# RWKV5 attention and a SwiGLU block: k and r without padding, a pair of heads in 96 columns, and zeros from a scale column

## The chip, the cores and the metric

The kernel runs on one core of one Trainium2 chip. The metric is the device time of one execution in microseconds (us), as the median over several executions. The span that a profile shows is about 1.7 us shorter than the time measured for the same execution, because it runs from the first to the last instruction. The granted clock is the share of its full speed at which TensorE was allowed to run, as the profile reports it.

Engines are named as in the profile: PE is TensorE's matmul stream, PEld its weight loads, DVE is VectorE, ACT is ScalarE, POOL is GpSimd and SP issues DMA. "L226" is a line of the kernel's source. Adding lines moves the numbers, so the same statement has other numbers in other kernels: `khat` is L226 before and L225 after.

## The reference

```python
B, H, S, D = 4, 8, 768, 48                    # r, k, v: (B, H, S, D); w, u: (H, D); all float32
for t in range(S):
    kt, vt, rt = k[:, :, t], v[:, :, t], r[:, :, t]
    cur = einsum('bhd,bhe->bhde', u[None] * kt, vt)
    y[:, :, t] = einsum('bhd,bhde->bhe', rt, state + cur)
    state = w[None, :, :, None] * state + einsum('bhd,bhe->bhde', kt, vt)
x = y.transpose(0, 2, 1, 3).reshape(B * S, H * D)              # 3072 x 384
g = x @ w_gate                                                 # 384 x 1536
out = (g * sigmoid(g) * (x @ w_val)) @ w_out                   # 1536 x 384
```

## The kernel before

The kernel cuts the sequence into chunks of 128 tokens. One step handles one chunk of one batch, 24 steps in all. Within a chunk the recurrence becomes matrix products: `khat` is k times a power of the decay, `rhat` is r divided by such a power, the scores are their product under a triangular mask, and the state `Z` is updated once a chunk. The term with `u` touches only the diagonal: `du` is the sum of r·k·u over a head, and `At` starts as the identity times `du`, before the scores are copied into it under the mask. Two heads go through TensorE together. Beside the steps runs the FFN (lines `gv` and `o_ps`), and in the first steps the FFN's weights, which arrive as 64-bit words, are rounded on ScalarE, VectorE and GpSimd.

Each head's 48 columns are padded to 64, so that a pair fills 128 columns, and after the transpose 128 partitions. The transposed k of each head sits in its own half of a tile `kT`, whose other half is zeroed once, at the start.

```python
    DP = 64                                   # D is 48, P is 128, H is 8, HP is 4
    wcol = cst.tile([P, HP], FP32, name="wcol")
    kscale = cst.tile([P, H, DP], FP32, name="kscale")
    r_ld = [cst.tile([P, H, DP], FP32, name=f"r_ld{i}") for i in range(2)]
    khat = [cst.tile([P, H, DP], FP32, name=f"khat{i}") for i in range(4)]
    kT = [cst.tile([P, HP, 2, P], FP32, name=f"kT{i}") for i in range(2)]
    # ... (cut) set-up:
    dve.tensor_scalar(held[:], wcol[:], W_LOW, W_HIGH, ALU.max, ALU.min)
    dve.tensor_copy(sq[:, 0, :], held[:])
    # ... (cut) powers of the decay by squaring, reciprocal, transposes into kscale and rscale
    for t in kT:
        for e in range(2):
            pool.memset(t[64 * e : 64 * e + 64, :, 1 - e, :], 0.0)

    def round_weights(count):                 # (cut) per chunk of weights:
            dve.tensor_scalar(dst, hi, -(1 << 31), None, ALU.bitwise_and)
            dve.scalar_tensor_tensor(dst, mag, 3, dst, ALU.logical_shift_left, ALU.bitwise_or)
            pool.tensor_tensor(dst, dst, low, ALU.add)

    def prepare(i):
        # ... (cut)
        pool.tensor_mul(khat[i % 4][:], kl[:], kscale[:])
        pool.tensor_mul(rhat[i % 2][:], rl[:], rscale[:])
        pool.tensor_mul(rk[:], rl[:, :, 0:D], kl[:, :, 0:D])
        pool.tensor_mul(rk[:], rk[:], ub[:])
        dve.tensor_reduce(du[:], rk[:], axis=AX.X, op=ALU.add)

    def turn(i):
        for nm, t in (("kT", khat[i % 4]), ("rT", rhat[i % 2])):
            tp = ps_a.tile([P, HP, P], FP32, name="tp", tag="a")
            for a in range(HP):
                pe.transpose(tp[:, a, :], t[:, 2 * a : 2 * a + 2, :].rearrange("p e d -> p (e d)"), ident[:])
            if nm == "kT":
                for e in range(2):
                    q = slice(64 * e, 64 * e + 64)
                    act.copy(kT[i % 2][q, :, e, :], tp[q])
            # ... (cut)

    def update(i):
        # ... (cut)
        for a in range(HP):
            pe.matmul(
                ps[:, a, :].rearrange("p (e d) -> p e d", e=2),
                kh[:, 2 * a : 2 * a + 2, :].rearrange("p e d -> p (e d)"),     # the weights
                v_pair(a),                                                     # (shortened) 2 x 48 columns of v
                start=True, stop=True, skip_group_check=True)

    prepare(0)
    for s in range(N + 2):                    # (cut: how many FFN pieces go in between)
        if 1 <= s <= N: diagonal(s - 1)       # At = ident * du, on GpSimd
        if s + 1 < N:   prepare(s + 1)
        if s < N:       turn(s)
        round_weights(1 if s else 0)
        # scores(s - 1), outputs(s - 2), update(s - 2)
        round_weights(1 if s > 1 else 0)
```

The order of instructions on each engine is fixed by this program order.

## Time and profile before

| what | value |
|---|---|
| time, median of 4 executions | 755.26 us (754.04 to 755.65) |
| span of the profiled execution | 752.1 us |
| PE busy | 704.4 us, 94% |
| POOL busy | 203.6 us, 27% |

The prediction below shows the page's shares, the chain and the windows of this kernel. Three more readings are kept here, because they are compared later.

The first is the timeline of the set-up of the kernel before: start us, duration us, engine, line, operation, tiles; in brackets the idle time before it and what ended that.

```profile
2.23 2.19 POOL L210 MEMSET kT<- 64x512 f32 x4
3.39 0.49 DVE L178 TENSOR_SCALAR held<-wcol 128x4 f32<-128x4 f32 x1 [1.60 <-DMA wcol<-in_w_dram]
3.92 0.52 DVE L179 COPY sq<-held 128x4 f32<-128x4 f32 x1
```

The two VectorE instructions touch four columns and last half a microsecond each. While they ran, GpSimd was filling `kT`.

The second is the chain of waits around the first state update after the start-up, and the transposes that follow it (start us, us, what):

```profile
142.73 0.86 PE u_ps L306 x8
...
146.21 0.87 PE tp L248 x8
```

Eight of each cost the same there. The third is the duration (min/median/max ns) of ScalarE's copies into `kT` between 130 and 740 us:

```profile
L254 ACT COPY kT<-tp x30: 579/580/582, 146.7 to 624.8; 64x512 f32<-64x512 f32 x30
```

### The profile page before, as it was taken

How to read it: one execution, taken by the hardware profiler on the slowest of the kernel's cores; microseconds unless marked ns; L12 is line 12 of the kernel's file. 1: busy time of each engine (PE TensorE's matmuls, PEld its weight loads, DVE VectorE, ACT ScalarE, POOL GpSimd, SP SyncE). 2: the span in 40 equal slices, each digit the busy share in tenths (PEclk: the TensorE clock that was granted, in tenths of full speed). 3: DMA queues.
4: the chain of work that ended last, by engine and by line, in shares of the span. 5: the costliest groups of instructions: out<-in, count | busy, mean ns of one | idle time of the engine just before them, and what ended most of it. 6: DMA issues, size and time to landing. Idle time of an engine off the chain costs nothing.

```text
span 752.1 us, 10222 instructions
## 1 busy us (share of the span) xinstructions
PE 704.4 (94%) x4298; PEld 563.0 (75%) x4298; DVE 218.1 (29%) x448; ACT 153.9 (20%) x305; POOL 203.6 (27%) x168
## 2 busy tenths in 40 slices
PE   2775978999999999999999999999999999999997
PEld 1654867878878778778778778778778778777773
DVE  4255654523222222223123213123213212212120
ACT  2541634311112111102111112111112112111110
POOL 5865667650303030303030303030302311000000
PEclk9988989999999999999999999999999999999999
DMA  8565555121102020102020201020100000000000
GB/s 213 112 152 147 165 161 156 32 43 33 32 11 43 1 43 11 31 11 43 1 53 1 44 11 31 12 42 5 38 22 1 23 12 2 12 10 2 10 11 24
DMA packets 85767, 33.98 MB, mean 45 GB/s; under 512 B 76368, under 2 KB 79568, under 8 KB 85712
## 3 DMA queue, kind: packets, MB, share of 16 engines
q1 hardware_dynamic: 82256, 28.52, 16.2%
q10 hardware_dynamic: 3456, 4.72, 1.8%
q8 instruction: 36, 0.59, 0.3%
q14 instruction: 19, 0.16, 0.1%
HBM read 28.51 MB, written 4.72 MB: 44 GB/s over the span
## 4 chain that ended last, share of the span: by engine, by line
PE 85%; POOL 6%; DVE 5%; issue 2%; ACT 1%; DMA 0%; SPq 0%; DVEq 0%; POOLq 0%
PE gv L332 48%; PE o_ps L351 25%; PE y_ps L293 4%; PE s_ps L263 4%; PE tp L248 2%; PE u_ps L306 2%; POOL At L239 2%; POOL rhat L227 1%; POOL khat L226 1%; POOL rk L229 1%; POOL rk L228 1%; DVE wv L156 1%; DVE wg L156 1%; DVE wv L155 1%; DVE wg L155 1%
## 5 line engine op out<-in xcount | busy, mean ns | idle before, releaser
L332 PE MATMUL gv<-xT,wg 128*128 128x256 f32 x864 | 217.5, 389 | 19.1 <-DVE hT L340 16.8
L332 PE MATMUL gv<-xT,wv 128*128 128x256 f32 x864 | 212.7, 383 | 0.0
L332 PEld LDWEIGHTS gv<-xT,wg 128*128 128x128 f32 x864 | 161.5, 193 | 50.4 <-issue 20.0
L351 PE MATMUL o_ps<-wo,hT 128*128 128x384 f32 x576 | 197.4, 487 | 0.6 <-ACT o_sb L357 0.6
L332 PEld LDWEIGHTS gv<-xT,wv 128*128 128x128 f32 x864 | 166.7, 193 | 23.5
L339 DVE TENSOR_TENSOR sg<-sg,gv 128x256 f32<-128x256 f32 x144 | 60.5, 420 | 359.3 <-ACT sg L338 359.3
L351 PEld LDWEIGHTS o_ps<-wo,hT 128*128 128x128 f32 x576 | 107.7, 190 | 62.0 <-ACT o_sb L357 1.2
L338 ACT ACTIVATE sg<-gv 128x256 f32<-128x256 f32 x144 | 55.3, 384 | 427.2 <-PE gv L332 427.2
L319 POOL TENSOR_TENSOR Z<-Z,wL 128x384 f32<-128x384 f32 x16 | 16.5, 1032 | 342.2 <-DVE Z L318 342.2
L340 DVE TENSOR_TENSOR hT<-sg,gv 128x256 f32<-128x256 f32 x144 | 60.5, 420 | 4.9
L239 POOL TENSOR_TENSOR At<-ident,du 128x1024 f32<-128x1024 f32 x24 | 45.5, 1898 | 37.6 <-PE y_ps L293 37.6
L263 PEld LDWEIGHTS s_ps<-rT,kT 128*128 128x128 f32 x384 | 50.4, 197 | 7.0 <-DVE At L267 0.7
L263 PE MATMUL s_ps<-rT,kT 128*128 128x128 f32 x384 | 51.0, 281 | 0.3 <-DVE At L267 0.3
L267 DVE COPY_PREDICATED At<-mask,s_ps 128x512 f32<-128x512 int32 x48 | 34.0, 732 | 41.5 <-PE s_ps L263 41.5
L231 DVE TENSOR_REDUCE du<-rk 128x8 f32<-128x384 f32 x24 | 13.3, 553 | 100.0 <-POOL rk L229 100.0
L293 PE MATMUL y_ps<-At,v_ld 128*32 128x128 f32 x768 | 36.7, 283 | 5.2 <-issue 2.8
L293 PEld LDWEIGHTS y_ps<-At,v_ld 128*32 128x32 f32 x768 | 30.4, 113 | 6.5 <-issue 3.6
L226 POOL TENSOR_TENSOR khat<-k_ld,kscale 128x512 f32<-128x512 f32 x24 | 30.5, 1271 | 5.4 <-ACT kscale L195 5.4
L227 POOL TENSOR_TENSOR rhat<-r_ld,rscale 128x512 f32<-128x512 f32 x24 | 30.6, 1274 | 2.0 <-ACT outside L218 2.0
L254 ACT COPY kT<-tp 64x512 f32<-64x512 f32 x48 | 27.9, 580 | 12.6 <-PE tp L248 11.3
L293 PE MATMUL y_ps<-rT,Z 128*32 128x128 f32 x480 | 30.1, 279 | 0.0
L293 PEld LDWEIGHTS y_ps<-rT,Z 128*32 128x32 f32 x480 | 19.3, 109 | 8.3 <-issue 7.8
(60 smaller groups left out, 318.4 us busy)
## 6 DMA issues: line engine op xcount, KB each, us to landing
k_ld<-in_k_dram SPq DMA_DIRECT2D x24, 192.0 KB, 3.1
r_ld<-in_r_dram SPq DMA_DIRECT2D x24, 192.0 KB, 3.5
w_bits<-in_moe_w_gate_dram SPq DMA_DIRECT2D x6, 768.0 KB, 4.6
w_bits<-in_moe_w_val_dram SPq DMA_DIRECT2D x6, 768.0 KB, 4.6
v_ld<-in_v_dram SPq DMA_DIRECT2D x48, 96.0 KB, 2.7
w_bits<-in_moe_w_out_dram SPq DMA_DIRECT2D x6, 768.0 KB, 4.3
out_dram<-o_sb ACTq DMA_DIRECT2D x24, 192.0 KB, 1.9
ub<-in_u_dram SPq DMA_DIRECT2D x1, 192.0 KB, 4.5
```

Of the source, the lines that this page charges most:

```text
L226: pool.tensor_mul(khat[i % 4][:], kl[:], kscale[:])
L227: pool.tensor_mul(rhat[i % 2][:], rl[:], rscale[:])
L239: pool.tensor_mul(At[i % 2][:], ident[:].unsqueeze(1).to_broadcast([P, H, P]), dus.pop(i)[:].unsqueeze(2).to_broadcast([P, H, P]),)
L254: act.copy(kT[i % 2][q, :, e, :], tp[q])
L263: pe.matmul(ps[:, n, :], kT[i % 2][:, a, e, :], turned[i][:, a, :], start=True, stop=True, skip_group_check=True,)
L267: dve.copy_predicated(At[i % 2][:, 4 * half : 4 * half + 4], mask[:].bitcast(INT32).unsqueeze(1).to_broadcast([P, HP, P]), ps[:],)
L293: pe.matmul(ps[32 * q : 32 * q + 32, cc, :], *rows[q][n], start=(n == 0), stop=(n == len(rows[q]) - 1), skip_group_check=True,)
L332: pe.matmul(gv[:, o, :].rearrange("p (i t) -> p i t", i=2), wt[:, c, P * f : P * (f + 1)], xT[:, 2 * g % NX : 2 * g % NX + 2, c, :], start ...
L338: act.activation(sg[:], gv[:, 0, :], AF.Sigmoid)
L339: dve.tensor_mul(sg[:], sg[:], gv[:, 0, :])
L340: dve.tensor_mul(hT[g][:, f, :], sg[:], gv[:, 1, :])
L351: pe.matmul(ps[:], hT[g][:, f, P * j : P * (j + 1)], wo[:, f, :], start=(f == 0), stop=(f == FC - 1),)
```

## The change

The padding goes: k, r and their scales are 8 x 48 = 384 columns wide, a pair of heads is 96 columns and 96 partitions. Then the two heads of a pair no longer start at partitions 0 and 64 but at 0 and 48. Instead of copying each half into a pre-zeroed tile, ScalarE copies all 96 rows twice, each time scaled by a column that is 1 on the rows of one head and 0 on the others. The memsets of `kT` go with it. The core of the diff:

```diff
-    kscale = cst.tile([P, H, DP], FP32, name="kscale")
+    kscale = cst.tile([P, H, D], FP32, name="kscale")
+    own = cst.tile([D2, 2], FP32, name="own")                 # D2 = 96
-    khat = [cst.tile([P, H, DP], FP32, name=f"khat{i}") for i in range(4)]
+    khat = [cst.tile([P, H, D], FP32, name=f"khat{i}") for i in range(4)]
-    kT = [cst.tile([P, HP, 2, P], FP32, name=f"kT{i}") for i in range(2)]
+    kT = [cst.tile([D2, HP, 2, P], FP32, name=f"kT{i}") for i in range(2)]
 ... (r_ld, k_ld, rhat, wcol, held, sq, Z, wL and the powers likewise; cut)
+    pool.memset(own[:], 1.0)
+    for step, base in ((-D, 0), (D, D - 1)):
+        pool.affine_select(
+            out=own[:], in_=own[:], compare_op=ALU.is_ge, fill=0.0,
+            base=base, pattern=[[step, 2]], channel_multiplier=1 if step < 0 else -1,
+        )
-    for t in kT:
-        for e in range(2):
-            pool.memset(t[64 * e : 64 * e + 64, :, 1 - e, :], 0.0)
 ... (cut)
                 for e in range(2):
-                    q = slice(64 * e, 64 * e + 64)
-                    act.copy(kT[i % 2][q, :, e, :], tp[q])
+                    act.activation(
+                        kT[i % 2][:, :, e, :], tp[0:D2], AF.Identity, scale=own[:, e : e + 1]
+                    )
 ... (cut)
-        ps = ps_a.tile([P, HP, 2 * D], FP32, name="u_ps", tag="a")
+        ps = ps_a.tile([D2, HP, D2], FP32, name="u_ps", tag="a")
         for a in range(HP):
             pe.matmul(
                 ps[:, a, :].rearrange("p (e d) -> p e d", e=2),
-                kh[:, 2 * a : 2 * a + 2, :].rearrange("p e d -> p (e d)"),
+                pair(kh, a),                                   # the same two heads, now 96 columns
```

More of the change, by code (lines that the diff above doesn't have):

```diff
@@ L49, in fast @@
     B, H, S, D = r.shape
-    DP = 64
+    D2 = 2 * D
     VW = 2 * D + 16
@@ L64, in fast @@
     dve, pool, act, pe, sp = nc.vector, nc.gpsimd, nc.scalar, nc.tensor, nc.sync
-    wcol = cst.tile([P, HP], FP32, name="wcol")
+    wcol = cst.tile([D2, HP], FP32, name="wcol")
     ub = cst.tile([P, H, D], FP32, name="ub")
-    kscale = cst.tile([P, H, DP], FP32, name="kscale")
-    rscale = cst.tile([P, H, DP], FP32, name="rscale")
-    wL = cst.tile([P, HP, 2 * D], FP32, name="wL")
-    sq = cst.tile([P, 8, HP], FP32, name="sq")
-    bad = cst.tile([P, HP], FP32, name="bad")
-    held = cst.tile([P, HP], FP32, name="held")
-    badc = cst.tile([P, 1], FP32, name="badc")
-    ones = cst.tile([P, 1], FP32, name="ones")
+    kscale = cst.tile([P, H, D], FP32, name="kscale")
+    rscale = cst.tile([P, H, D], FP32, name="rscale")
+    own = cst.tile([D2, 2], FP32, name="own")
+    wL = cst.tile([D2, HP, 2, D], FP32, name="wL")
+    sq = cst.tile([D2, 8, HP], FP32, name="sq")
+    bad = cst.tile([D2, HP], FP32, name="bad")
+    held = cst.tile([D2, HP], FP32, name="held")
+    badc = cst.tile([D2, 1], FP32, name="badc")
+    ones = cst.tile([D2, 1], FP32, name="ones")
     ident = cst.tile([P, P], FP32, name="ident")
@@ L83, in fast @@
     xT = cst.tile([P, NX, CC, P], FP32, name="xT")
-    Z = [cst.tile([P, HP, 2 * D], FP32, name=f"Z{b}") for b in range(B)]
-    r_ld = [cst.tile([P, H, DP], FP32, name=f"r_ld{i}") for i in range(2)]
-    k_ld = [cst.tile([P, H, DP], FP32, name=f"k_ld{i}") for i in range(2)]
+    Z = [cst.tile([D2, HP, D2], FP32, name=f"Z{b}") for b in range(B)]
+    r_ld = [cst.tile([P, H, D], FP32, name=f"r_ld{i}") for i in range(2)]
+    k_ld = [cst.tile([P, H, D], FP32, name=f"k_ld{i}") for i in range(2)]
     v_ld = [cst.tile([P, HP, VW], FP32, name=f"v_ld{i}") for i in range(4)]
-    khat = [cst.tile([P, H, DP], FP32, name=f"khat{i}") for i in range(4)]
-    rhat = [cst.tile([P, H, DP], FP32, name=f"rhat{i}") for i in range(2)]
+    khat = [cst.tile([P, H, D], FP32, name=f"khat{i}") for i in range(4)]
+    rhat = [cst.tile([P, H, D], FP32, name=f"rhat{i}") for i in range(2)]
     At = [cst.tile([P, H, P], FP32, name=f"At{i}") for i in range(2)]
-    kT = [cst.tile([P, HP, 2, P], FP32, name=f"kT{i}") for i in range(2)]
+    kT = [cst.tile([D2, HP, 2, P], FP32, name=f"kT{i}") for i in range(2)]
     def load(i):
@@ L98, in load @@
         for src, dst in ((k, k_ld[i % 2]), (r, r_ld[i % 2])):
-            sp.dma_start(out=dst[:, :, 0:D], in_=src[b, :, rows, :].rearrange("h t d -> t h d"))
+            sp.dma_start(out=dst[:], in_=src[b, :, rows, :].rearrange("h t d -> t h d"))
     def load_v(i):
@@ L158, in round_weights @@
             load_weights()
-    pool.memset(wcol[:], 1.0)
-    for t in k_ld + r_ld:
-        dve.memset(t[:, :, D:DP], 0.0)
     for t in v_ld:
@@ L166, in fast @@
     for e in range(2):
-        sp.dma_start(out=wcol[64 * e : 64 * e + D, :], in_=w.rearrange("(a e) d -> e d a", e=2)[e])
+        sp.dma_start(out=wcol[D * e : D * e + D, :], in_=w.rearrange("(a e) d -> e d a", e=2)[e])
     load(0)
@@ L181, in fast @@
         dve.tensor_mul(sq[:, l, :], sq[:, l - 1, :], sq[:, l - 1, :])
-    pw = two.tile([P, HP, P + 1], FP32, name="pw", tag="hT")
-    ipw = two.tile([P, HP, P], FP32, name="ipw", tag="hT")
+    pw = two.tile([D2, HP, P + 1], FP32, name="pw", tag="hT")
+    ipw = two.tile([D2, HP, P], FP32, name="ipw", tag="hT")
     dve.memset(pw[:, :, P : P + 1], 1.0)
@@ L187, in fast @@
         n = 1 << l
-        f = sq[:, l, :].unsqueeze(2).to_broadcast([P, HP, n])
+        f = sq[:, l, :].unsqueeze(2).to_broadcast([D2, HP, n])
         dve.tensor_mul(pw[:, :, P - 2 * n : P - n], pw[:, :, P - n : P], f)
@@ L191, in fast @@
     for src, dst in ((pw[:, :, 1 : P + 1], kscale), (ipw[:], rscale)):
-        t_ps = ps_a.tile([P, HP, P], FP32, name="t_ps", tag="a")
+        t_ps = ps_a.tile([P, HP, D2], FP32, name="t_ps", tag="a")
         for a in range(HP):
-            pe.transpose(t_ps[:, a, :], src[:, a, :], ident[:])
+            pe.transpose(t_ps[:, a, :], src[:, a, :], ident[0:D2, 0:D2])
         act.copy(dst[:].rearrange("p h d -> p (h d)"), t_ps[:].rearrange("p a x -> p (a x)"))
-    pool.memset(wL[:], 0.0)
-    for e in range(2):
-        q = slice(64 * e, 64 * e + 64)
-        dve.tensor_copy(
-            wL[q, :, D * e : D * (e + 1)], sq[q, 7, :].unsqueeze(2).to_broadcast([64, HP, D])
-        )
+    dve.tensor_mul(
+        wL[:], sq[:, 7, :].unsqueeze(2).unsqueeze(3).to_broadcast([D2, HP, 2, D]),
+        own[:].unsqueeze(1).unsqueeze(3).to_broadcast([D2, HP, 2, D]),
+    )
     pool.memset(mask[:], 1.0)
@@ L207, in fast @@
     )
-    for t in kT:
-        for e in range(2):
-            pool.memset(t[64 * e : 64 * e + 64, :, 1 - e, :], 0.0)
     dve.tensor_tensor(bad[:], held[:], wcol[:], ALU.not_equal)
@@ L227, in prepare @@
         pool.tensor_mul(rhat[i % 2][:], rl[:], rscale[:])
-        pool.tensor_mul(rk[:], rl[:, :, 0:D], kl[:, :, 0:D])
+        pool.tensor_mul(rk[:], rl[:], kl[:])
         pool.tensor_mul(rk[:], rk[:], ub[:])
@@ L242, in diagonal, with pair @@
         )
+    def pair(t, a):
+        return t[:, 2 * a : 2 * a + 2, :].rearrange("p e d -> p (e d)")
     def turn(i):
@@ L247, in turn @@
             for a in range(HP):
-                pe.transpose(
-                    tp[:, a, :], t[:, 2 * a : 2 * a + 2, :].rearrange("p e d -> p (e d)"), ident[:]
-                )
+                pe.transpose(tp[0:D2, a, :], pair(t, a), ident[:])
             if nm == "kT":
                 for e in range(2):
-                    q = slice(64 * e, 64 * e + 64)
-                    act.copy(kT[i % 2][q, :, e, :], tp[q])
-            else:
-                turned[i] = three.tile([P, HP, P], FP32, name=nm, tag=nm)
-                act.copy(turned[i][:], tp[:])
+                    act.activation(
+                        kT[i % 2][:, :, e, :], tp[0:D2], AF.Identity, scale=own[:, e : e + 1]
+                    )
+            else:
+                turned[i] = three.tile([D2, HP, P], FP32, name=nm, tag=nm)
+                act.copy(turned[i][:], tp[0:D2])
     def scores(i, half):
@@ L315, in update @@
         if c == 0:
-            dve.tensor_mul(z[:], ps[:], wL[:])
+            dve.tensor_mul(z[:], ps[:], wL[:].rearrange("p a e d -> p a (e d)"))
         else:
             dve.tensor_add(z[:], ps[:], z[:])
-            pool.tensor_mul(z[:], z[:], wL[:])
+            pool.tensor_mul(z[:], z[:], wL[:].rearrange("p a e d -> p a (e d)"))
     hT = {}
```

## The prediction

> **What bounds the kernel now.** I read the page first, for the engines' shares and the chain that ended last, then the table of windows, then the chain in order of time for the first 150 us, then the waits, and last the instruction durations of single lines. The page says TensorE is busy nearly all the time, but not where the rest of the chain lies:
>
> ```profile
> PE 704.4 (94%) x4298; PEld 563.0 (75%) x4298; DVE 218.1 (29%) x448; ACT 153.9 (20%) x305; POOL 203.6 (27%) x168
> ...
> PE 85%; POOL 6%; DVE 5%; issue 2%; ACT 1%; DMA 0%; SPq 0%; DVEq 0%; POOLq 0%
> ```
>
> So about 13% of the span, some 100 us, is chain that is not TensorE. The table of windows (width; then busy us of PE, PEld, DVE, ACT and POOL, with counts; granted clock; DMA share; GB/s) says where:
>
> ```profile
> 50.00:60.00 10.00, 7.46 (x34) 6.10 (x35) 6.66 (x10) 3.79 (x6) 5.45 (x5) 0.83 0.59 147
> 60.00:70.00 10.00, 4.46 (x51) 3.53 (x50) 2.91 (x5) 2.45 (x4) 7.27 (x7) 0.92 0.50 117
> ...
> 300.00:400.00 100.00, 100.00 (x559) 79.64 (x558) 25.39 (x56) 16.19 (x36) 21.81 (x18) 1.00 0.12 26
> ```
>
> Before about 105 us TensorE starves; from about 125 us on it never does. The kernel is two stages with different bounds. In the first, the chain in order of time (start us, us, what) repeats this cycle, about 14.4 us long where no TensorE piece joins it:
>
> ```profile
> 46.07 1.90 POOL At L239
> 47.97 1.22 POOL khat L226
> 49.19 1.22 POOL rhat L227
> 50.41 0.97 POOL rk L228
> ...
> 51.45 1.00 POOL rk L229
> 52.48 0.55 DVE du L231
> 53.03 0.87 DVE wv L155
> ```
>
> After it come the rest of the weight rounding on VectorE, one weight add on GpSimd (POOL, L157), and the next `At`. The waits of the same stage (16 to 105 us: total, times, longest) confirm that VectorE waits for POOL in every cycle, so each microsecond of those five POOL products is on the path:
>
> ```profile
> DVE du L231 <- POOL rk L229: 50.7, 8, 8.3
> ```
>
> In the second stage the chain is TensorE back to back, and only TensorE's pitch counts. Durations of two of its lines there (142 to 200 us; min/median/max ns):
>
> ```profile
> L306 PEld LDWEIGHTS u_ps<-v_ld,khat x24: 190/192/192, 142.4 to 195.5; 128*128 128x128 f32 x24
> L306 PE MATMUL u_ps<-v_ld,khat x24: 246/275/275, 142.6 to 195.6; 128*128 128x96 f32 x24
> L248 PEld LDWEIGHTS tp<-ident,khat x8: 140/140/142, 145.7 to 164.6; 128*128 128x128 f32 x8
> ```
>
> **What the Trainium skill says.** "TensorE: Matmul & The Clock Gate", the section on LDWEIGHTS: a weight load's time goes with its columns, P/1.2 ns, and not with the contraction rows. The trace agrees: 128 columns take a median of 192 ns here (u_ps) and the 32-column loads of y_ps 109 to 110, so 82 ns for 96 columns, 0.86 ns each. "GPSIMD Engine Reference", section 3.1: a two-input product is bound by one shared read port at about 2.5 cycles of a 1.2 GHz clock per element. The trace agrees: 512 columns take 1272 ns (khat, rhat), 384 take 1000 (rk), so 2.1 ns a column. "ScalarE: Activation LUTs", "What ACT_TABLE_LOAD costs": an ACTIVATE pays about 93 ns for each per-partition pointer operand; no run so far shows it. The same page, "Table sets", puts identity in every set; the changed program indeed has the same two table loads.
>
> **The change part by part.**
>
> (1) `khat` and `rhat` shrink from 512 to 384 columns. Their step in the chain should fall from 1.23 us to that of `rk`, 0.965: 0.265 us each, 0.53 us a cycle. In the first stage the pairs that start at 16.4, 22.7, 33.5, 48.0, 62.4, 78.4 and 97.3 us are on the chain, and the very first `rhat` too: 7 x 0.53 + 0.27 = **4.0 us** on the path. Later pairs lie beside TensorE: nothing.
>
> (2) The set-up. Four POOL memsets of kT (2.19 us), that of wL (0.42) and VectorE's four of k and r (0.6) go; POOL stood idle 5.38 us before the first `khat`, so that gives nothing. On the chain are: the memset of wcol ahead of its load (about 0.15 us by the start times; the other engines start at 0.8), the four transposes of the second scale, 96 columns moved in place of 128 at the cold pitch of about 0.22 us a transpose (1.09 to about 0.87), and ScalarE's copy (0.587 to the 0.479 of another 384-column copy). Together **0.45 us**. The reciprocal (3.35 us) keeps 512 columns a partition.
>
> (3) The state update (L306) loads 96 columns of weights in place of 128. Eight instructions take 0.86 us on the chain, 108 ns each, although only 96 columns move; the score products with 128 moved columns take 1.78 us for 16, 111 ns. So I take the update to be bound by its weight load (its matmuls show a median of 275 ns against a minimum of 246, which I read as waiting for weights). With 96 columns both sides come to about 80 to 84 ns: 24 to 26 ns an instruction, 0.2 us an update. 20 updates exist, 5 run before 105 us; 15 x 0.2 = **3.0 us** on the path.
>
> (4) The transposes (L248, 8 in 0.87 us, 109 ns each) also load 96 columns, but their load is shorter already, 140 ns against 192, and they still move 128 columns of the identity. I count **0**. Score and output products contract 96 rows in place of 128, at the same columns: **0**. Tile shapes are unchanged in the program (128 by 128 and 128 by 32), so no new switch of mode.
>
> (5) `kT` goes from 48 ScalarE copies of 64x512 (580 ns) to 48 scaled copies of 96x512. Perhaps +93 ns each, 4.5 us of ScalarE work. Its reader is the score product of the *next* step, a cycle of 14 to 18 us later, and ScalarE is 20% busy: **0** on the path.
>
> (6) The loads of k and r carry the same bytes from the same 192-byte rows; DMA lies off the chain (0%).
>
> Sum: 4.0 + 0.45 + 3.0 = 7.5 us; 755.1 - 7.5 = 747.6. I round to **747.8**.
>
> **Rivals.** *A, the POOL saving is not passed on.* If VectorE's fixed order made a score product or a weight load the wait that ends last, `du` would start earlier and the masked copy after it would wait instead. For it: VectorE's order is fixed, and ScalarE's rounding copies also wait on VectorE. Against: the score products are done about 1.7 us before their masked copies (38.8 and 40.5 us), and they move up with `rhat`. Then 751. *B, transposes are bound by their weight load.* If 96 columns help there too, each of some 120 later transposes gains up to 27 ns, 3.2 us more: 744.5. Against: the 140 ns load. *C, the update is bound by something else* (a fixed pitch near 108 ns, say): part 3 is nothing, 750.7. For it: no 96-column load exists in this trace. *D, the clock.* Three TensorE pieces of the first stage ran at a lower granted clock: 12 instructions of gv took 5.23, 4.89 and 4.21 us instead of 2.6 to 2.9. Shifting the idle time moves where such a window falls, some 2 us either way. *E, ScalarE becomes a wait*: it would need to lose a whole cycle of slack; I give it little.
>
> **Range and chances.** The largest doubts are D (2 us), B (-3) and A or C (+3 each). That makes a standard deviation near 3 us: range **744.0 to 752.0**. Faster by over 2% means below 740.0, which needs more than twice the sum; 0.02. Slower by over 2% needs a new stall of 15 us; 0.01. Within 2%: 0.97.
>
> **What would show it.** In the changed profile: khat and rhat near 1.0 us each and a first-stage cycle near 13.9 us in place of 14.4; TensorE back to back from about 100 us on; the update's weight load near 165 ns and eight of its instructions in about 0.66 us; transposes still 0.87 us for eight; kT copies of 0.58 to 0.68 us with nobody waiting for them. The prediction is wrong if the cycle keeps 14.4 us with a new releaser (A), if the update's eight keep 0.86 (C), if the transposes' eight fall to about 0.66 (B), or if the score or output products get slower with 96 rows, which I count as nothing.

## The result, and the profile after

The changed kernel took 746.19 us (median of 4, 746.14 to 746.27) against 755.26 us. The ratio is 0.9883, with a 95% interval of 0.9866 to 0.9900: within 2%, as predicted, and inside the range. A ratio here is the mean time of one kernel's fast runs over that of the other's of the same rounds, so it is not quite the ratio of the medians. The results are correct.

The page of the kernel after, first the engines' busy time, then the shares of the chain that ended last:

```profile
PE 699.4 (94%) x4298; PEld 557.3 (75%) x4298; DVE 216.7 (29%) x443; ACT 152.8 (21%) x305; POOL 188.2 (25%) x165
...
PE 83%; POOL 7%; DVE 6%; issue 3%; ACT 1%; DMA 0%; SPq 0%; DVEq 0%; POOLq 0%
```

POOL lost 15.4 us of work and PE 5.0 us, and the span fell by 7.7 us (752.1 to 744.4): neither engine's busy time gives the answer, since most of POOL's work lay beside TensorE. The shape of the chain has not changed.

The chain of the kernel after in one cycle of the start-up stage:

```profile
42.89 1.89 POOL At L238
44.78 0.95 POOL khat L225
45.73 0.95 POOL rhat L226
46.69 0.97 POOL rk L227
...
47.72 1.01 POOL rk L228
...
48.75 0.55 DVE du L230
```

`khat` and `rhat` now take a step of 0.95 us each instead of 1.22. The next `At` starts at 56.77 us: the cycle is 13.9 us, where it was 14.4. It has the same members in the same order. The waits between 16 and 105 us (total us, times, longest us) name the same releaser:

```profile
DVE du L230 <- POOL rk L228: 42.5, 7, 7.8
```

Before, the same wait was 50.7 us over 8 times. The timeline of the set-up of the kernel after:

```profile
3.23 0.17 DVE L183 TENSOR_SCALAR held<-wcol 96x4 f32<-96x4 f32 x1 [2.01 <-DMA wcol<-in_w_dram]
3.43 0.17 DVE L184 COPY sq<-held 96x4 f32<-96x4 f32 x1
```

The two small VectorE instructions take 0.17 us each in place of 0.49 and 0.52. No GpSimd memset runs beside them any more.

Then the durations between 130 and 740 us (min/median/max ns), of the update's weight loads and products, the transposes' loads and the scaled copies:

```profile
L307 PEld LDWEIGHTS u_ps<-v_ld,khat x112: 163/165/165, 137.1 to 575.0; 128*96 128x96 f32 x112
L307 PE MATMUL u_ps<-v_ld,khat x112: 246/248/248, 137.3 to 575.0; 128*96 128x96 f32 x112
...
L250 PEld LDWEIGHTS tp<-ident,khat x60: 124/126/129, 140.3 to 616.1; 128*96 128x96 f32 x60
...
L253 ACT ACTIVATE kT<-tp,own x30: 671/677/683, 141.3 to 617.2; 96x512 f32<-96x512 f32 x30
```

And the same two pieces of the chain as shown of before:

```profile
137.50 0.68 PE u_ps L307 x8
...
140.78 0.87 PE tp L250 x8
```

The update's eight instructions fell from 0.86 to 0.68 us; the eight transposes still take 0.87 us, although their weight load is shorter too.

Laying the two traces side by side along the chain gives a ledger for the whole 7.7 us of span. The first `rhat` starts at 11.82 us instead of 13.06: 1.24 us from the set-up. The eighth of the start-up's `At` starts at 124.47 instead of 130.01: 5.54 us, so 4.30 came from the eight cycles in between. The next `y_ps` starts at 133.01 instead of 138.25: 5.24 us, so 0.30 was given back there: the twelve `gv` instructions in between took 4.51 us instead of 4.21. From it to the end the gain grows to 7.7 us, so 2.46 came from the stretch where TensorE runs back to back and 14 updates of 0.18 us less (2.52 us) lie.

### The profile page after: what moved, and what is told of

Its sections match the earlier page's. It is cut to its first block, busy times and chain, and to the rows that moved or that the text cites. A ratio compares the mean times of both kernels' runs of the same rounds, so it can differ in the third digit from the quotient of the medians.

```text
span 744.4 us, 10214 instructions
## 1 busy us (share of the span) xinstructions
PE 699.4 (94%) x4298; PEld 557.3 (75%) x4298; DVE 216.7 (29%) x443; ACT 152.8 (21%) x305; POOL 188.2 (25%) x165
## 4 chain that ended last, share of the span: by engine, by line
PE 83%; POOL 7%; DVE 6%; issue 3%; ACT 1%; DMA 0%; SPq 0%; DVEq 0%; POOLq 0%
PE gv L333 47%; PE o_ps L352 25%; PE y_ps L294 4%; PE s_ps L264 4%; PE tp L250 2%; POOL At L238 2%; PE u_ps L307 1%; POOL rk L228 1%; POOL rk L227 1%; POOL khat L225 1%; POOL rhat L226 1%; DVE At L268 1%; DVE wg L157 1%; DVE wg L156 1%; DVE wv L157 1%
## 5 line engine op out<-in xcount | busy, mean ns | idle before, releaser
L320 POOL TENSOR_TENSOR Z<-Z,wL 96x384 f32<-96x384 f32 x16 | 16.4, 1028 | 348.0 <-DVE Z L319 348.0
L264 PEld LDWEIGHTS s_ps<-rT,kT 96*128 96x128 f32 x384 | 49.9, 196 | 7.6 <-ACT kT L253 0.8
L264 PE MATMUL s_ps<-rT,kT 96*128 96x128 f32 x384 | 50.5, 279 | 0.8 <-ACT kT L253 0.5
L253 ACT ACTIVATE kT<-tp,own 96x512 f32<-96x512 f32 x48 | 30.2, 677 | 11.4 <-PE tp L250 10.4
L294 PE MATMUL y_ps<-rT,Z 96*32 96x128 f32 x480 | 30.2, 278 | 0.0
L294 PEld LDWEIGHTS y_ps<-rT,Z 96*32 96x32 f32 x480 | 19.3, 109 | 8.3 <-issue 7.8
L225 POOL TENSOR_TENSOR khat<-k_ld,kscale 128x384 f32<-128x384 f32 x24 | 23.8, 993 | 6.1 <-ACT kscale L200 6.1
L358 ACT COPY o_sb<-o_ps 128x384 f32<-128x384 f32 x24 | 11.5, 478 | 64.7 <-PE o_ps L352 64.7
```

What stands on the lines that cost most here:

```text
L253: act.activation(kT[i % 2][:, :, e, :], tp[0:D2], AF.Identity, scale=own[:, e : e + 1])
L264: pe.matmul(ps[:, n, :], kT[i % 2][:, a, e, :], turned[i][:, a, :], start=True, stop=True, skip_group_check=True,)
L294: pe.matmul(ps[32 * q : 32 * q + 32, cc, :], *rows[q][n], start=(n == 0), stop=(n == len(rows[q]) - 1), skip_group_check=True,)
L320: pool.tensor_mul(z[:], z[:], wL[:].rearrange("p a e d -> p a (e d)"))
```

## The experiments

Twelve runs were made, in three groups that each shared executions of the kernel before on the same chip (medians of it 755.19, 754.94 and 754.05 us). Unless it says otherwise, the ratio is against the kernel before. Theory: the gain is the sum of the update's narrower loads, the narrower GpSimd products, and the set-up. The rivals are those of the prediction: a part of the sum is worth nothing, or the gain is the clock.

### The changed kernel once more

No edit; it is the control for the runs on the same chip.

> The changed kernel once more, as the control of this set. First measured ratio 0.988 (746.2 us). Both theories (the gain is the shorter GpSimd products plus a shorter set-up plus the narrower weight load of the update; or mostly a luckier fall of the granted clock) expect 0.986 to 0.991 here; the second also allows another value on another chip.

Measured: 745.55 us (744.90 to 746.21), ratio 0.9880 [0.9865, 0.9895]. The executions fall into two groups, at 744.9 and 746.2 us; so do those of the kernel before, at 754.1 and 755.3. The profiled execution was of the lower group, the one of the result above was not, and they can be compared. Their chains agree up to 118.1 us. The next twelve FFN instructions, first of the kernel after in the upper group, then of this run in the lower one:

```profile
118.07 4.51 PE gv L333 x12
```

```profile
118.11 2.83 PE gv L333 x12
```

The update that follows starts at 137.50 us in the one and at 136.27 in the other, 1.23 us apart. The granted clock from 118 to 123 us is 0.66 in the one and 1.00 in the other. So between these two executions the spacing of the groups is whether TensorE's lower granted clock falls on these instructions. A difference of about one microsecond between two medians can be no more than which group the executions fell into; for such a size the trace is read instead.

### GpSimd products over 512 columns again

The products `khat` and `rhat` run over 512 contiguous columns (128 of them padding, zeroed once by VectorE in the set-up), everything else stays as in the kernel after.

```diff
-        pool.tensor_mul(khat[i % 4][:], kl[:], kscale[:])
-        pool.tensor_mul(rhat[i % 2][:], rl[:], rscale[:])
+        pool.tensor_mul(khat_w[i % 4][:], k_w[i % 2][:], kscale_w[:])      # tiles of 512 columns,
+        pool.tensor_mul(rhat_w[i % 2][:], r_w[i % 2][:], rscale_w[:])      # used through views of 384
```

> The changed kernel with the two GpSimd products khat and rhat made over 512 columns a partition again (128 columns of zeros behind the 384), all else as changed. Theory: eight pairs and the first rhat lie on the chain of the first stage, 0.27 us a product, so 4.2 to 4.8 us come back: about 750.6 us, ratio to the kernel before 0.994; the cycle goes from 13.9 to 14.4 us. Rival (the products are hidden and the gain is elsewhere): 746 us.

Measured: 750.94 us (750.87 to 751.98), ratio 0.9954 [0.9940, 0.9967]; 5.6 us more than the control by the ratios (0.0074 of 755), 5.4 by the medians. The chain of this run:

```profile
46.79 1.22 POOL khat L232
48.01 1.22 POOL rhat L233
```

The steps are 1.22 us again and the `At` that precedes them starts at 44.89, the one after at 59.72. The whole time says somewhat more than the 4.30 us of the ledger, and the traces say why. The eighth `At` starts at 129.16 us against 124.55 in the control, 4.61 later, of which 0.09 comes from the set-up (the first `rhat` at 11.93 against 11.84). That leaves 4.5 us for the products. The remaining 1.3 us arise between this `At` and the next update (12.87 us against 11.56 in the control and 12.86 in the kernel after): the spacing of the groups. Rival A (the saving is not passed on) falls.

### Update loads of 128 columns again

The update takes 128 contiguous columns of `khat` as weights, of which 96 count.

```diff
-                pair(kh, a),
+                khat_w[i % 4][:, D2 * a : D2 * a + P],
```

> The changed kernel with the state update loading 128 columns of weights again (the 32 columns behind a pair are the next pair's; their rows of the sum are not read), all else as changed. Theory: the update is bound by its weight load, so eight instructions take 0.86 us in place of 0.68, and 14 to 15 updates on TensorE's back-to-back stretch give 2.5 to 2.7 us back: about 748.8 us. Rival (a fixed pitch; the shorter eight come from the 96 rows of the result or from elsewhere): no change, 746.

Measured: 748.53 us (747.12 to 749.51), ratio 0.9915 [0.9902, 0.9929]; 2.6 us more than the control by the ratios, 3.0 by the medians. Durations between 130 and 740 us:

```profile
L310 PEld LDWEIGHTS u_ps<-v_ld,khat x112: 190/192/192, 136.6 to 577.0; 128*128 128x128 f32 x112
```

The load is back at 192 ns, the products' median at 275 ns and the eight at 0.86 us, while the start-up cycle is unchanged. The five executions spread over 2.4 us, so the traces are the better measure. From the start of the seventh update to the end of the span it takes 609.5 us in the kernel before and 609.7 in this run, with 128 columns, but 607.1 to 607.2 in the kernel after, in the control and in the run with wide products, with 96. So the narrower load is worth 2.4 to 2.6 us there, whichever group an execution falls into. Rival C (the update has a fixed pitch) falls.

### The load's columns alone, in the kernel before

To see the slope without the rest of the change, the kernel before loads 112 columns of weights in the update (the last 16 of the 128 are padding).

```diff
-                kh[:, 2 * a : 2 * a + 2, :].rearrange("p e d -> p (e d)"),
+                kh[:, 2 * a : 2 * a + 2, :].rearrange("p e d -> p (e d)")[:, 0 : P - 16],
```

> The kernel before with one part alone: its update loads 112 columns of weights in place of 128 (the pad of the second head left out), padded layout otherwise kept. Theory (weight load bounds the update, 0.85 ns a column): 14 ns less an instruction, 0.11 us an update, 14 to 15 updates on the path, 1.5 us: ratio 0.998. Eight instructions take about 0.75 us, the weight load about 178 ns. Rival (no gain until the load is shorter than the moved 96 columns, or a fixed pitch): ratio 1.000 and 0.86 us.

Measured: 753.11 us (752.94 to 753.98), ratio 0.9979 [0.9966, 0.9993], 1.6 us less. Durations between 130 and 740 us:

```profile
L308 PEld LDWEIGHTS u_ps<-v_ld,khat x112: 177/178/178, 143.5 to 582.5; 128*112 128x112 f32 x112
```

The eight take 0.77 us. So 96, 112 and 128 columns give 165, 178 and 192 ns a load, and 0.68, 0.77 and 0.86 us for eight instructions: 0.84 ns a column of load, and 0.7 ns a column on the path, with the 96 moved columns unchanged. So the update follows its load's columns and not the columns that it moves. One thing stays unseparated: the columns of the load are also the rows of the result, so the result shrank with the load in all of these runs. The transposes also got 96 rows in place of 128 and still take 0.87 us, so fewer rows alone did not shorten them.

### The memsets put back

The four GpSimd memsets return, filling tiles that are overwritten later.

```diff
+    for t in At:
+        for e in range(2):
+            pool.memset(t[64 * e : 64 * e + 64, 0:HP, :], 0.0)
```

> The changed kernel with four GpSimd memsets of 64x512 put back where those of kT stood (into At, which is written later anyway). My prediction held that they cost nothing, since GpSimd is idle then. Theory now: while GpSimd works, VectorE's two tiny set-up operations on one SBUF source (held, and the copy of it) take about 0.5 us each in place of 0.17, and they are on the chain, so the first khat starts 0.6 to 0.7 us later and the time is about 746.9 us. Rival (those two were slow for another reason, such as 128 partitions in place of 96): both stay at 0.17 us and nothing moves.

Measured: 746.82 us (746.75 to 747.66), ratio 0.9894 [0.9878, 0.9909]. By the ratios that is 1.1 us over the control, but the intervals overlap: the whole time does not settle it. The timeline of the set-up does:

```profile
2.38 2.19 POOL L214 MEMSET At<- 64x512 f32 x4
...
3.23 0.24 DVE L183 TENSOR_SCALAR held<-wcol 96x4 f32<-96x4 f32 x1 [2.01 <-DMA wcol<-in_w_dram]
3.51 0.52 DVE L184 COPY sq<-held 96x4 f32<-96x4 f32 x1
```

The same two instructions on the same tiles take 0.24 and 0.52 us beside the memsets and 0.17 and 0.17 without them, and the first `rhat` starts 0.44 us later (12.26 instead of 11.82). Moreover, they end when a memset ends. The packed trace has each memset by itself: 0.52 us, with 0.04 us to the next. In this run the second and third end at 3.45 and 4.01; `held` ended at 3.48 and the copy at 4.03. In the kernel before, the third and fourth end at 3.86 and 4.42; `held` ended at 3.89 and the copy at 4.45. The Trainium skill, "SBUF — State Buffer", section "Who interferes with whom", gives the rule: copies and scalar operations of VectorE can run in a mode that takes the port pair shared with GpSimd, whoever issues first keeps it for its whole instruction, and the other fully blocks. The trace agrees, down to the ends of the memsets. Not every instruction is held: the next ones on VectorE, products with two sources (`sq`), took 0.16 us each beside the fourth memset.

### The scaled copies twice

Each scaled copy into `kT` is issued twice, to load ScalarE.

```diff
-                for e in range(2):
+                for e in (0, 0, 1, 1):
```

> The changed kernel with each scaled copy of kT on ScalarE done twice, 48 more instructions of 0.68 us, 32 us more of ScalarE work. Theory: their reader comes a step later, so the dearer copies (677 ns against 580) are beside the path and even doubled cost under 1 us: 746 to 747. Rival (ScalarE's copies bind the score products in the first stage, and the gain could have been larger with plain copies): 10 us or more are lost.

Measured: 746.88 us (745.51 to 746.96), ratio 0.9889 [0.9874, 0.9904], against 0.9880 of the control: no resolved difference. The durations, with twice as many of them in the same stretch:

```profile
L253 ACT ACTIVATE kT<-tp,own x60: 672/682/684, 141.2 to 618.6; 96x512 f32<-96x512 f32 x60
```

Over the whole run ScalarE spent 62.9 us on 96 of these copies, half of it in vain, and no wait in this trace is put down to them. (In the kernel after, TensorE's loads waited for such a copy once, 0.8 us, and in the control two of the copies, 0.46 and 0.68 us, lie on the chain; doubling them did not make that grow.) What the scaled copy costs ScalarE (677 ns instead of 580) is hidden within what these runs resolve; rival E falls.

### The reduction moved to the end of the step

The chain points past the change. VectorE waits 42.5 us in the start-up for GpSimd's last product, because `du` stands ahead of the weight rounding in its fixed order, though its value is needed only in the next step. The edit moves `du` behind the step's other work, and changes nothing else.

```diff
-        du = three.tile([P, H], FP32, name="du", tag="du")
-        dve.tensor_reduce(du[:], rk[:], axis=AX.X, op=ALU.add)
-        dus[i] = du
+        rks[i] = rk
 ... (cut: the main loop, after the second round_weights)
+        if s + 1 < N:
+            reduce(s + 1)                     # the same tensor_reduce
```

> The changed kernel with VectorE's reduction du moved from right after its GpSimd products to the end of the step, nothing else. In the first stage VectorE stands and waits for the products of GpSimd in every cycle, and GpSimd then waits for VectorE. Theory P (only the order makes them alternate): the two overlap, the cycle falls from 13.9 us towards GpSimd's own 9 us or until TensorE binds, and 15 to 30 us go: 716 to 731 us. Theory Q (VectorE's weight operations can't run while GpSimd works, as in e4): they only take turns in another order, and the gain is under 5 us.

Measured: 724.16 us (723.83 to 725.20), ratio 0.9596 [0.9583, 0.9609]. That is 21.4 us less than the control by the ratios, more than twice what the change itself gained. The table of windows of the start-up (width; then busy us of PE, PEld, DVE, ACT and POOL, with counts; granted clock; DMA share; GB/s), first of the kernel after, then of this one:

```profile
40.00:50.00 10.00, 7.13 (x32) 5.50 (x31) 2.21 (x3) 5.76 (x9) 7.52 (x6) 0.86 0.52 140
```

```profile
40.00:50.00 10.00, 8.56 (x54) 7.16 (x56) 8.43 (x12) 6.86 (x11) 9.92 (x8) 1.00 0.68 177
```

VectorE and GpSimd no longer take turns: GpSimd is busy 9.92 of 10 us and the cycle falls to 10.0 us (`At` at 38.51 and at 48.54). In the kernel after VectorE alone waited 42.5 of the 89 us from 16 to 105 for GpSimd's last product, so the layout change could only trim the products, while the order of the program held the rest. The granted clock rises to 1.00 in this window as well, and TensorE's busy time over the whole run falls from 699.4 to 692.3 us for the same 4298 instructions. So some of the 21 us may be the clock's; no run separates it from the overlap.

### The same move in the kernel before

The same edit on the kernel before tells whether the two changes add.

```diff
-        dve.tensor_reduce(du[:], rk[:], axis=AX.X, op=ALU.add)
+        rks[i] = rk                           # reduced at the end of the step, as above
```

> The kernel before with the same move of du. It tells what the layout change is worth when the first stage is bound otherwise. Theory P: also 15 to 30 us faster than before, and the layout change on top is worth 2.6 us (the update) plus at most 4 us (products, while GpSimd is the bound). Theory Q: under 5 us.

Measured: 727.76 us (726.91 to 728.06), ratio 0.9639 [0.9626, 0.9653]. The layout change on top of it is worth 3.2 us by the ratios (0.0043 of 755), 3.6 by the medians, less than half of what it is worth alone. The two traces say where the rest went. The seventh `At` starts at 88.02 us in the run above and at 93.14 in this one, 5.1 us apart. The seventh update starts at 116.34 and 116.54, only 0.2 apart. In between, the run above has on its chain an instruction of 6.6 us that the next section shows; the longest of that line and tile here takes 2.16. From the seventh update to the end it is 607.1 against 609.5 us, the update's part. So the products and the set-up did save time, and most of it was lost where only the one run has that block.

### A block in VectorE, and three attempts at it

With the reduction moved, one thing stands out. The timeline of that run (VectorE's instruction first, then GpSimd's):

```profile
86.58 6.63 DVE L156 TENSOR_SCALAR wo<-w_bits 128x768 int32<-128x768 int32 x1
```

```profile
86.24 1.82 POOL L158 TENSOR_TENSOR wo<-wo,w_low 128x768 int32<-128x768 int32 x1
88.02 1.89 POOL L241 TENSOR_TENSOR At<-ident,du 128x1024 f32<-128x1024 f32 x1
89.88 0.99 POOL L230 TENSOR_TENSOR khat<-k_ld,kscale 128x384 f32<-128x384 f32 x1
90.83 1.00 POOL L231 TENSOR_TENSOR rhat<-r_ld,rscale 128x384 f32<-128x384 f32 x1
91.80 0.99 POOL L232 TENSOR_TENSOR rk<-r_ld,k_ld 128x384 f32<-128x384 f32 x1
92.87 1.20 POOL L233 TENSOR_TENSOR rk<-rk,ub 128x384 f32<-128x384 f32 x1
```

An instruction of this line and shape that took 0.56 us at 112.28 us in the same trace lasted 6.63 here, until 93.21. GpSimd's first five instructions follow each other without a gap from 86.24 to 92.79, where the first gap lies. All of VectorE's chain stands behind it, and TensorE runs dry (7.32 of 10 us busy from 90 to 100). It looks like the block of the set-up, but through a run of instructions rather than one. Of the next three kernels the first and the third try to get rid of it, and the second tests the place of the reduction.

First, the product with `u` went to VectorE, which leaves GpSimd one instruction less a cycle:

```diff
-        pool.tensor_mul(rk[:], rk[:], ub[:])
 ... (cut: in reduce)
+        dve.tensor_mul(rks[i][:], rks[i][:], ub[:])
```

> The variant with du late, and the product of rk with u moved from GpSimd to VectorE as well, just ahead of du. GpSimd is busy 99% of the first stage there and VectorE 55 to 85%. Theory R (the stage is now bound by GpSimd's busy time): GpSimd loses 1.0 us a step, five to seven steps, so 3 to 6 us go: 718 to 721 us. Theory S (a VectorE operation on two SBUF sources waits while GpSimd works, as the weight operations seem to): the product takes well over its 0.5 us, and the time stays within 2 us of 724 or grows.

Measured: 723.03 us, ratio 0.9590 [0.9574, 0.9606]: four executions between 722.94 and 723.98, and one, the profiled one, of 715.23. The median is what theory S forecast. In the fast execution no VectorE instruction takes longer than 2.7 us after the set-up (the same `wo` operation takes 1.20 us at 78.59), and TensorE is busy 19.52 of the 20 us from 80 to 100. The slower four have no trace. That their 8 us hang on how the two engines' instructions happen to meet is likely from the blocks in the neighbouring runs, but not shown.

Second, the moved reduction stood ahead of the second rounding instead of behind it, to see whether its exact place matters:

```diff
+        if s + 1 < N:
+            reduce(s + 1)
         round_weights(1 if s > 1 else 0)
```

> The variant with du late, but put ahead of the second weight rounding of the step in place of behind it. If the place of du matters only by not standing ahead of the first rounding, the time stays at 724 within 1.5 us; if the last steps of the first stage, where VectorE is the chain, were held by du, 1 to 3 us change.

Measured: 723.29 us (722.86 to 724.55), ratio 0.9591 [0.9575, 0.9607]. The place doesn't matter within the noise, as expected.

Third, I held that only one-source operations, which can take the port pair, are blocked for so long, and gave the `wo` operation a form with two sources, with `u`'s product still on VectorE:

```diff
-            dve.tensor_scalar(dst, hi, -(1 << 31), None, ALU.bitwise_and)
+            if c == 2:                        # the chunks of wo
+                dve.scalar_tensor_tensor(dst, hi, -(1 << 31), hi, ALU.bitwise_and, ALU.bitwise_and)
+            else:
+                dve.tensor_scalar(dst, hi, -(1 << 31), None, ALU.bitwise_and)
```

> The variant e9 (du late, product with u on VectorE) with one VectorE operation of the rounding of wo in another form: the sign is cut out by a two-source operation on the same operand twice, not by a one-source operation. In e7 the one-source form over wo (six of them) took 2134 ns in the mean and once 6.63 us, ending only where GpSimd paused, against 658 ns in the kernel before; the same operation over wg and wv, whose pattern differs, took 942 ns in all kernels. e9 fell in two groups, 715.2 once and 722.9 to 724.0 four times. Theory (that one-source form stands until GpSimd is idle, and whether it meets a gap is luck): no operation over 3 us is left, the runs agree within 2 us, near 714 to 718 us. Rival (the two groups come from the granted clock or DMA): still two groups, near 723.

Measured: 723.77 us (722.91 to 724.65), ratio 0.9592 [0.9579, 0.9605]. The theory is refuted, and no execution near 715 us came up. The timeline of this run has the block on another instruction, which has two sources in SBUF:

```profile
80.56 7.83 DVE L227 TENSOR_TENSOR rk<-rk,ub 128x384 f32<-128x384 f32 x1
```

GpSimd ran from 79.78 to 87.97 us without a gap; in the fast execution above, the same product took 0.55 us at 81.38.

### The two-source form with the product left on GpSimd

The same form of the `wo` operation on top of the moved reduction, so that VectorE has no product of its own to be blocked.

```diff
+        pool.tensor_mul(rk[:], rk[:], ub[:])             # back on GpSimd
 ... (cut: in reduce)
-        dve.tensor_mul(rks[i][:], rks[i][:], ub[:])
```

> The variant e7 (du late alone) with the same other form of that operation. Theory: the block of 6.6 us at 86 us, which lies on the chain of e7, goes, and 4 to 7 us with it: 717 to 720 us. Rival: 724 as e7.

Measured: 721.82 us (720.54 to 722.12), ratio 0.9565 [0.9551, 0.9579], the best median of all. It gains 2.3 us over the moved reduction alone, by both measures, not the 4 to 7 that the theory asked for: blocks of 5.4 and 7.0 us remain on that same operation, now with two sources. This, too, speaks against the theory.

So in these traces three kinds of VectorE instruction stood behind a run of GpSimd instructions: the one-source `wo` operation (6.63 us), its two-source form (7.0) and the two-source product (7.83). Which one it is changes with small shifts. What decides it stays open, and so does how to get the 715 us reliably.

One kind never did, and these experiments passed it over. The same source line rounds `wg` and `wv` by the same one-source operation, with its 768 columns in three pieces instead of two. From the groups of the run with the moved reduction (busy us, mean ns):

```profile
L156 DVE TENSOR_SCALAR wg<-w_bits 128x768 int32<-128x768 int32 x6 | 5.7, 942 | 0.0
```

The six of `wo` took 2134 ns in the mean there, and 550 where nothing held them. Those of `wg` and `wv` took at most 0.96 us in all fourteen traces, although GpSimd was busy 9.92 of 10 us beside some of them. They are slower, but were never held. No run gave `wo` that form.

## Why the prediction was right, point by point

The prediction was 747.8 us against a median of 746.19; its sum was a saving of 7.5 us, against 7.7 in the two profiles and 9.1 in the medians. The profiled executions were timed at 753.81 and 746.18 us, which is the lower group of before and the upper of after, so their difference is about one spacing of the groups (1.2 us) smaller than that of the medians. The prediction had that as its rival D, with 2 us either way.

| term | predicted us | in the traces us | undone alone, by ratios us |
|---|---|---|---|
| GpSimd products | 4.0 | 4.30, of which 0.30 given back | 5.6 (4.5 in the trace) |
| set-up | 0.45 | 1.24 | 1.1 (memsets only; 0.44 in the trace) |
| update's loads | 3.0 | 2.46 | 2.6 (the same in the trace) |
| sum | 7.5 | 7.7 | 9.3 |

That the sum comes so close is partly luck: the set-up was taken 0.8 us too low and the update 0.5 too high.

- **Products.** Mechanism and size hold. The steps went to 0.95 us, the cycle to 13.9. I had seven pairs and a first `rhat`; an eighth pair was on the path and brought 0.54 us, and the clock took 0.30 us back. Of the seven, the fifth brought only 0.16 us in place of 0.53 (the lead of the `At` before it was 3.73 us, of the one after it 3.89). That the size fits to 0.3 us is therefore in part luck, too.
- **Set-up.** This is the term that was mis-sized, by a factor of nearly three. The step that failed is the sentence that the memsets' removal "gives nothing", because GpSimd had idle time afterwards. I asked whether GpSimd was on the path, and it wasn't; I did not ask whom it kept waiting. It blocked two VectorE instructions that are on the path: 0.67 us (0.49 + 0.52 less 0.17 + 0.17). The run with memsets put back shows 0.42 of this (0.24 + 0.52 less 0.34), where the first of the two met the end of a memset sooner. The rest, some 0.57, is close to the 0.45 that I had counted. The transposes of the scale went from 1.09 to 0.87 us, ScalarE's copy from 0.59 to 0.48, and the load of `wcol` was issued 0.14 us earlier (0.80 instead of 0.94). The page of the skill that says so was there to be read; I had not looked at it for a change that only takes things away.
- **Update.** Mechanism right: the load's columns set the pitch (the 112-column run). The size was a little high: 0.18 us an update in place of 0.2, and 14 of them on the back-to-back stretch in place of 15.
- **Transposes.** Nothing, as predicted; their eight stayed at 0.87 us. Rival B falls.
- **Scaled copies.** 677 ns, against 580 + 93 expected, and off the path (the doubled copies). The Trainium skill, "ScalarE: Activation LUTs", section "What ACT_TABLE_LOAD costs", gives about 93 ns for a pointer operand; the scaled copy measured 97 ns more than the plain copy, though with 96 partitions in place of 64. It agrees.
- **Scores and outputs** with 96 rows took the same time, as I had counted.
- One detail of what would show it was wrong: I wrote that TensorE would run back to back from about 100 us. In the trace it does only from 120 us (7.81 of 10 us busy from 110 to 120).
- Three slips without consequence. By the page's shares 15% of the span, not 13, is chain that is not TensorE (100 - 85). The sum gives 747.6, and 747.8 is not a rounding of it. The 2.5 cycles an element of a two-input GpSimd product stand in section 2.1 of "GPSIMD Engine Reference"; section 3.1 has about 2.6. The slope read from the trace, 2.1 ns a column, is 2.55 cycles at that page's 1.2 GHz and fits both.

## What to carry to other kernels

Ask what an engine that is off the path does to the other engines, not only to itself: GpSimd work in "idle time" made two tiny VectorE instructions on the path three times as long. In a chain in which two engines alternate, narrowing the operations gives what their steps lose (here 4.3 to 4.5 us, 0.6%), but first look whether the fixed program order makes one wait for a value that is needed later; moving one reduction gave 3.6% in the kernel before, without the change. A matmul that moves fewer columns than its weights have (96 and 128 here) can be bound by its load, so padding of the weights cost TensorE time here.

## What the Trainium skill lacked or had wrong

- "SBUF — State Buffer", "Who interferes with whom": right about the set-up (0.17 us becoming 0.24 to 0.52 beside memsets, ending within 0.03 us of a memset's end). It also states what the third attempt ran into: a VectorE instruction with two SBUF inputs contends with a GpSimd instruction that reads SBUF. And it states that one with at most one SBUF input, outside the two-port modes, doesn't contend, which the `wg` and `wv` operations fit (at most 0.96 us). But it speaks of a block for the whole instruction of the other. The runs show one that lasts through a whole run of back-to-back GpSimd instructions: 6.63 us over five of them, 7.83 us over the run from 79.78 to 87.97 us, ended only after a gap. The memsets, 0.04 us apart, let VectorE in between two of them; the products, each of which starts some 0.04 us before the one ahead of it ends, did not. This difference is not on the page.
- "TensorE: Matmul & The Clock Gate", section on LDWEIGHTS: the slope agrees (165, 178, 192 ns for 96, 112, 128 columns, 0.84 ns each, against 1/1.2), the value doesn't. P/1.2 gives 80, 93 and 107 ns, and the durations are some 85 ns longer. What comes near it is the pitch of the update's instructions (0.68, 0.77 and 0.86 us for eight: 85, 96 and 108 ns). The load of a transpose doesn't follow these sizes: 140 ns for 128 columns and 126 for 96. Neither this section nor the one on the PE-mode transpose has a time for it.
